# Row maxima and V's bound through TensorE in 16 bits, and a constant moved into exp's bias

## The chip, the cores and the metric

One Trainium2 chip; the kernel runs on one of its cores. The metric is the time of one execution on the device, in microseconds. A core has TensorE (PE in the profile; its weight loads are shown apart as PEld), VectorE (DVE), ScalarE (ACT), GpSimd (POOL) and SyncE (SP, which issues the DMAs here).

## What is computed

Attention over 16 heads of 64 columns (2 batches of 8), with the queries averaged in pairs, and then two MLPs over the 1152 rows that come out, all in float32:

```
q_pool = q.reshape(B, H, S // 2, 2, D).mean(axis=3)
scores = matmul(q_pool, k^T) / sqrt(D)
scores = scores - max(scores, axis=-1)
attn   = exp(scores);  attn = attn / (sum(attn) + 1e-09)
x      = matmul(attn, v)                       # then heads side by side: 1152 x 512
h = x @ w_in;   x = (max(h, 0) + alpha * min(h, 0)) @ moe_w_out
h = x @ w2_in;  out = (P(h) / (Q(h) + 1e-06)) @ moe2_w_out
```

S is 1152, so a head has 576 pooled queries against 1152 keys. The change lies in the attention.

## The kernel before

Heads are worked two at a time (8 pairs). Near-float32 precision comes from splitting operands in a high and a low part and multiplying the parts. A head's keys are taken in NT = 9 tiles of 128, its queries in NJ = 5 blocks of 128 (the last one of 64).

Before a pair's scores are made, the maximum over the keys is found for every query. `max_mm` (line 435) multiplies query blocks with the keys in three chunks of 384 (tiles m0, m1, m2 in PSUM, nine steps a pair); ScalarE's `max_relu` (441) and VectorE's `max_1` (444) and `max_2` (449) reduce them to `nm`. `max_split` (463 to 467) then makes the negative maximum of 5 or 9 query blocks at once, adds a constant (exp's factor 2^14, as PSH / SC), and splits it in a high and a low part `mt` of two columns per block. `max_rows` (481) turns each block's two columns into two rows with a TensorE transpose against the float32 identity, and `max_put` (497) copies these rows to partitions 64 and 65 of `QQ`, from where they are two more rows of the second matmul of the scores, against two rows of ones in `K2`. So the scores come out with the maximum already subtracted. For the first head `first_m` (511) does the work of `max_rows` and `max_put`.

`score` (523) makes the scores of one key tile: four matmuls to a PSUM buffer `st`, of which there are two. `p_exp` (534) is ScalarE's exp of it to `PF`, `p_lo` (540) the low part `PL` on GpSimd (on VectorE for some tiles), and `av` (552 to 556) multiplies both, in 16 bits, with V's high and low part: fifteen small matmuls a tile, some three tiles after the scores.

V is scaled by a power of two. `v_abs` (360) sums |V| of a head per partition to `AM`; `v_max` (372) turns the two heads' columns into a row by a product with the identity, in float32; `v_scale` (377 to 382) takes the maximum and makes a power of two and its inverse from it; `v_scale2` (385) spreads the two over all partitions by a product with a row of ones, in float32; `v_scale3` (390) copies them.

The order on each engine is the order of the program: every step is entered with a time on a scale of one key tile per unit (`at(time, fn, ...)`), and `emit` sorts by it. The engines run these lists in order, with semaphores between them. During the last pair the weights of the MLPs are unpacked as well (lines 128 to 156) by ScalarE, VectorE and GpSimd. `init_1` and `init_2` set constants at the start; `warm` (245) runs products of the identity with itself.

Of the kernel before, what the change touches and what calls it, by code (L numbers as in the profile page):

```python
# [11 lines left out]
F32 = mybir.dt.float32  # L12
F32R = mybir.dt.float32r
F16 = mybir.dt.float16
BF16 = mybir.dt.bfloat16
I32 = mybir.dt.int32
I64 = mybir.dt.int64
AF = mybir.ActivationFunctionType
ALU = mybir.AluOpType
AX = mybir.AxisListType  # L20

P = 128
# [3 lines left out]
def attention_then_two_mlps(  # L26
# [14 lines left out]
    nc = tc.nc  # L41
    NPAIR, _, _, SQ = qT.shape
    BH, D = 2 * NPAIR, P // 2
# [6 lines left out]
    HALF = SQ // 2  # L50
# [5 lines left out]
    SC = 0.5 / math.sqrt(D)  # L56
    PSH = 14.0 * math.log(2.0)
# [135 lines left out]
    for f in range(NF):  # L193
# [10 lines left out]
    hold = actx.enter_context(tc.tile_pool(name="hold", bufs=1))  # L204
# [5 lines left out]
    small = actx.enter_context(tc.tile_pool(name="small", bufs=2))  # L210
# [3 lines left out]

    CW = 384
    EVEN, ODD = 2, 3
    K1 = [[(early, hold, early)[i].tile([P, SK + CW], F32R, name=f"K1_{o}{i}")
           for i in range((EVEN, ODD)[o])] for o in range(2)]  # L220
    QQ = [[(early, hold, early)[i].tile([P, 2, SQP], F32R, name=f"QQ_{o}{i}")
           for i in range((EVEN, ODD)[o])] for o in range(2)]
    K2 = [[(early, hold)[i].tile([D + 2, SK], F32R, name=f"K2_{o}{i}") for i in range(2)] for o in range(2)]
    V16 = [hold.tile([P, NT, 130], F16, name=f"V16_{i}") for i in range(2)]
    NPB = 6
    PF = [hold.tile([P, SQP], F32, name=f"PF_{i}") for i in range(NPB)]
    PL = [hold.tile([P, SQP], F16, name=f"PL_{i}") for i in range(NPB)]
    ident = hold.tile([P, P], F32, name="ident")
    ones1 = hold.tile([1, P], F32, name="ones1")
    PAD = SQP - SQ  # L230

    def init_1():
        for o in range(2):
            for qq in QQ[o]:
                z = slice(0, PAD) if o else slice(SQ, SQP)
                nc.gpsimd.memset(qq[:, 0, z].bitcast(F32), 0.0)
        make_identity(nc, ident)
        nc.gpsimd.memset(ones1, 1.0)


    def warm(n):
# [5 lines left out]
    def init_2():  # L247
        for i in range(2):
            for o in range(2):
                e = nc.vector if o > i else nc.gpsimd  # L250
                e.memset(K2[o][i][D:D + 2, :].bitcast(F32), 1.0)
        for i in range(NPB):
            nc.vector.memset(PF[i][:, SQ:SQP], 0.0)
            nc.vector.memset(PL[i][:, SQ:SQP], 0.0)
        for i in range(2):
            nc.gpsimd.memset(V16[i][:, :, 0:1], 1.0)

    def of(bufs, n):
        p, o = divmod(n, 2)
        return bufs[o][p % len(bufs[o])]  # L260
# [4 lines left out]
    KR, QR, QS, QH, QL, KH, KL, VR, VS, AM, X, NM, O, ST, TS = ({} for _ in range(15))  # L265
# [21 lines left out]
    def k_hi(p, c=slice(0, SK)):  # L287
        if p not in KH:
            KH[p] = prep.tile([P, SK + CW], F32R, tag="kh", name="kh")
        nc.scalar.activation(out=KH[p][:, c], in_=KR[p][:, c], func=AF.Copy)  # L290

    def k_diff(p):
        nc.gpsimd.tensor_tensor(
            out=KH[p][:, SK:SK + CW], in0=KH[p][:, CW:2 * CW].bitcast(F32),
            in1=KH[p][:, 0:CW].bitcast(F32), op=ALU.subtract)

# [41 lines left out]
    def first_kh():  # L338
        for c in (slice(0, 2 * CW), slice(2 * CW, SK)):
            nc.scalar.activation(out=of(K1, 0)[0:D, c], in_=KR[0][0:D, c], func=AF.Copy)  # L340
# [4 lines left out]
    def first_kd():  # L345
        k = of(K1, 0)
        nc.vector.tensor_tensor(
            out=k[:, SK:SK + CW], in0=k[:, CW:2 * CW].bitcast(F32), in1=k[:, 0:CW].bitcast(F32),
            op=ALU.subtract)
# [14 lines left out]
    VC = NJ * (D + 1)  # L364

    def v_max(p):
        if p:
            AM[p, 1] = O[2 * p - 2]
        else:
            AM[p, 1] = psum.tile([P, 512], F32, tag="o", name="vt")  # L370
        for o in range(2):
            nc.tensor.matmul(AM[p, 1][0:1, VC:VC + P], lhsT=AM[p][:, o:o + 1], rhs=ident,
                             start=p == 0 and o == 0, stop=o == 1, skip_group_check=True)

    def v_scale(p):
# [6 lines left out]
        nc.vector.reciprocal(out=g[:, 4:5], in_=g[:, 3:4])  # L382

    def v_scale2(p):
        nc.tensor.matmul(AM[p, 1][:, VC + P:VC + P + 2], lhsT=ones1, rhs=AM[p, 0][:, 3:5], start=p == 0,
                         stop=True, skip_group_check=True)

    def v_scale3(p):
# [3 lines left out]
    def v_scale_at(t1, t2, p):  # L392
        at(t1, v_max, p)
        at(t1 + 0.2, v_scale, p)
        at(t2, v_scale2, p)
        at(t2 + 0.2, v_scale3, p)
# [20 lines left out]
    NJ2 = 2 * NJ - 1  # L417
# [42 lines left out]
    def max_split(p, j0, j1):  # L460
        w = j1 - j0
        nm1 = small.tile([P, NJ2], F32, tag="nm1", name="nm1")
        nc.vector.tensor_reduce(
            out=nm1[:, 0:w], in_=NM[p][:, j0:j1, :], axis=AX.X, op=ALU.max, negate=True)
        TS[p, j0] = mt = small.tile([P, 2, NJ2], F32R, tag="mt", name="mt")
        nc.vector.tensor_scalar(mt[:, 0, 0:w], nm1[:, 0:w], PSH / SC, None, op0=ALU.add)
        nc.vector.scalar_tensor_tensor(
            out=mt[:, 1, 0:w], in0=nm1[:, 0:w], scalar=PSH / SC, in1=mt[:, 0, 0:w].bitcast(F32),
            op0=ALU.add, op1=ALU.subtract)

    def max_rows(p, j0, j1):
        mt = TS.pop((p, j0))
        parts = {}
        for tag, k0, k1 in (("m0", 0, NJ - 1), ("m1", NJ - 1, NJ), ("m2", NJ, NJ2)):
            k0, k1 = max(k0, j0), min(k1, j1)
            if k0 < k1:
                tp = psum.tile([P, 512], F32, tag=tag, name="mtp")
                for j in range(k0, k1):  # L480
                    nc.tensor.transpose(  # L481
                        out=tp[0:2, (j - k0) * P:(j - k0 + 1) * P], in_=mt[:, :, j - j0].bitcast(F32),
                        identity=ident)
                parts[k0] = tp, (k1 - k0) * P
        TS[p, j0] = parts

# [14 lines left out]
    def max_fin_at(time, *a):  # L501
        at(time, max_split, *a)
        at(time + (0.621 if a[0] == 0 else 1.129), max_rows, *a)
        at(time + (0.922 if a[0] == 0 else 1.4), max_put, *a)


    def first_m():
        mt, q = TS.pop((0, 0)), of(QQ, 0)
        st = stp.tile([P, 2, 512], F32, tag="st", name="mst")
        for j in range(NJ):  # L510
            nc.tensor.transpose(
                out=st[0:2, j // 4, j % 4 * P:(j % 4 + 1) * P], in_=mt[:, :, j].bitcast(F32), identity=ident)
        nc.scalar.activation(out=q[D:D + 2, 1, 0:512], in_=st[0:2, 0, :], func=AF.Copy)
        nc.scalar.activation(out=q[D:D + 2, 1, 512:SQ], in_=st[0:2, 1, 0:SQ - 512], func=AF.Copy)

# [11 lines left out]
    def buf(n, t):  # L527
        return (n * NT + t) % NPB

    def top(u):  # L530
        return PF[u].bitcast(BF16).rearrange("p (q two) -> p q two", two=2)[:, :, 1]

    def p_exp(n, t):
        nc.scalar.activation(  # L534
            out=PF[buf(n, t)][:, 0:SQ].rearrange("p (h q) -> p h q", h=2),
            in_=ST.pop((n, t))[:, :, 0:HALF], func=AF.Exp, scale=SC)

    def p_lo(n, t, e):
        u = buf(n, t)
        e.tensor_tensor(out=PL[u][:, 0:SQ], in0=PF[u][:, 0:SQ], in1=top(u)[:, 0:SQ], op=ALU.subtract)  # L540

    def av(n, t):
        i = n % 2
        u = buf(n, t)
        if t == 0:
            O[n] = psum.tile([P, 512], F32, tag="o", name="o")
        for j in range(NJ):
            o = O[n][:, j * (D + 1):(j + 1) * (D + 1)]
            ph = top(u)[:, j * P:(j + 1) * P]
            pl = PL[u][:, j * P:(j + 1) * P]  # L550
            first, last = t == 0 and j == 0, t == NT - 1
            nc.tensor.matmul(o, lhsT=ph, rhs=V16[i][:, t, 0:D + 1], start=first, stop=False,  # L552
                             skip_group_check=True)
            nc.tensor.matmul(o[:, 1:D + 1], lhsT=ph, rhs=V16[i][:, t, D + 1:2 * D + 1], start=False,  # L554
                             stop=False, skip_group_check=True)
            nc.tensor.matmul(o, lhsT=pl, rhs=V16[i][:, t, 0:D + 1], start=False, stop=last,  # L556
                             skip_group_check=True)
# [96 lines left out]
    for p in range(NP):  # L654
# [21 lines left out]
        for o in range(2):  # L676
            n = 2 * p + o
# [167 lines left out]
    def mt(s):  # L845
        return S2 * NP + 1 + 3.3 * s


    def dly(s):
        if s < PASS_B:  # L850
            return 2.5
        return 3.5

    for s, u in enumerate(steps):
# [23 lines left out]
        e = mt(s + dly(s))  # L878
# [18 lines left out]
    t = PASS_B + 1.8  # L897
# [48 lines left out]
```

## Time and profile before

| | |
|---|---|
| median of 3 runs | 686.64 us (685.75 to 687.48) |
| the profiled execution | 682.94 us, of which the span of the instructions is 681.1 |
| TensorE / VectorE busy | 647.6 us (95%) / 516.2 us (76%) |
| ScalarE / GpSimd busy | 485.4 us (71%) / 403.8 us (59%) |
| mean granted clock of TensorE | 0.987 |
| chain that ended last | TensorE 64%, VectorE 20%, ScalarE 7% |

Busy time of TensorE counts matmuls whose ends are modelled and which overlap in its pipeline: two rows of matmuls are told apart by their starts. In a timeline, pieces of one line that follow each other without a gap stand in one row with their count; its length reaches from the first start to the last end.

### The profile page before, as it was taken

The numbers are of one execution on the slowest core, as the hardware profiler recorded it, in microseconds if no ns is written. First come the engines' busy times: TensorE is split into PE (matmuls) and PEld (weight loads), VectorE is DVE, ScalarE is ACT, GpSimd is POOL, SyncE is SP. The second block draws the span as 40 slices with busy tenths as digits, with TensorE's granted clock in tenths as the row PEclk, the third lists the DMA queues.
The fourth block names the chain that finished last, engine by engine and source line by source line (L and its number), as shares of the span: only waits on it lengthen the run. The fifth ranks groups of instructions, "written<-read, shape, count | busy, mean of one in ns | idle before, by whom it ended". The sixth has DMA issues, their size and how long they took to land.

```text
span 681.1 us, 13756 instructions
## 1 busy us (share of the span) xinstructions
PE 647.6 (95%) x5226; PEld 580.3 (85%) x5226; DVE 516.2 (76%) x944; ACT 485.4 (71%) x916; POOL 403.8 (59%) x352
## 2 busy tenths in 40 slices
PE   6888999999999889999999999999999999999997
PEld 4767898988989779999999999999887779999995
DVE  7677867778678998998992149996788877667774
ACT  5666686776867756665764368888788888778774
POOL 8454776857766766685663226785465655444442
PEclk9699999999999979999999999999999999999999
DMA  8979659496593224343330005640320010001001
GB/s 221 197 197 226 129 159 216 125 230 129 160 207 103 69 89 155 125 153 125 140 136 35 1 1 195 231 161 31 124 93 31 1 47 0 2 1 47 1 1 46
DMA packets 21537, 73.96 MB, mean 109 GB/s; under 512 B 3232, under 2 KB 3232, under 8 KB 21472
## 3 DMA queue, kind: packets, MB, share of 16 engines
q1 hardware_dynamic: 21472, 73.10, 37.7%
q8 instruction: 41, 0.67, 0.4%
q14 instruction: 24, 0.20, 0.1%
HBM read 47.72 MB, written 2.36 MB: 74 GB/s over the span
## 4 chain that ended last, share of the span: by engine, by line
PE 64%; DVE 20%; ACT 7%; issue 5%; DMA 2%; POOL 1%; SPq 1%; POOLq 0%; DVEq 0%; ACTq 0%
PE hp L184 20%; PE acc L810 18%; PE st L523 10%; PE m L435 6%; DVE bits L138 3%; PE o L552 3%; PE o L554 2%; PE o L556 2%; DVE bits L133 2%; DVE ring L146 2%; DVE g L791 1%; DVE g L776 1%; DVE hp L789 1%; DVE b L787 1%; PE mtp L481 1%
## 5 line engine op out<-in xcount | busy, mean ns | idle before, releaser
L540 POOL TENSOR_TENSOR PL<-PF 128x576 f16<-128x576 f32 x106 | 134.8, 1284 | 77.1 <-ACT PF L534 75.3
L799 POOL TENSOR_TENSOR gl<-g,gh 128x384 fp32r<-128x384 f32 x96 | 104.8, 1092 | 72.2 <-ACT gh L795 58.4
L534 ACT ACTIVATE PF<-st 128x576 f32<-128x576 f32 x144 | 92.2, 650 | 43.9 <-PE st L523 42.2
L810 PE MATMUL acc<-woh,gl 128*128 128x512 f32 x288 | 114.3, 397 | 3.2 <-POOL gl L799 3.2
L810 PE MATMUL acc<-woh,gh 128*128 128x512 f32 x288 | 113.3, 393 | 2.2 <-ACT m L841 1.7
L810 PE MATMUL acc<-wol,gh 128*128 128x512 f32 x288 | 113.2, 393 | 0.0
L523 PE MATMUL st<-QQ,K 128*128 128x288 f32 (+1 forms) x576 | 105.6, 311 | 0.4 <-ACT PF L534 0.4
L769 POOL TENSOR_TENSOR b<-a,b 128x384 f32<-128x384 f32 x48 | 48.9, 1019 | 84.4 <-ACT b L757 83.3
L523 PEld LDWEIGHTS st<-QQ,K 128*128 128x128 f32 (+1 forms) x576 | 90.3, 197 | 2.6 <-ACT V L407 1.3
L184 PE MATMUL hp<-xh,wih 128*128 128x384 f32 x384 | 83.7, 340 | 0.0
L184 PE MATMUL hp<-xl,wih 128*128 128x384 f32 x384 | 83.2, 338 | 0.0
L184 PE MATMUL hp<-xh,wil 128*128 128x384 f32 x384 | 83.0, 338 | 0.0
L435 PE MATMUL m<-K,QQ 128*128 128x384 f32 x234 | 70.5, 372 | 8.9 <-DVE nm L444 5.1
L552 PE MATMUL o<-V,PF 128*128 128x65 f16 x720 | 76.7, 195 | 1.6 <-DVE x L567 1.4
L556 PE MATMUL o<-V,PL 128*128 128x65 f16 x720 | 75.5, 193 | 1.9 <-DVE PL L540 1.7
L554 PE MATMUL o<-V,PF 128*128 128x64 f16 x720 | 76.0, 196 | 0.0
L184 PEld LDWEIGHTS hp<-xh,wih 128*128 128x128 f32 x384 | 69.4, 188 | 7.5
L552 PEld LDWEIGHTS <-PF 128*128 128x128 bf16 x720 | 66.5, 98 | 9.1 <-issue 2.1
L795 ACT ACTIVATE gh<-g 128x384 fp32r<-128x384 f32 x96 | 49.9, 520 | 31.8 <-DVE g L760 21.8
L556 PEld LDWEIGHTS <-PL 128*128 128x128 f16 x720 | 67.6, 100 | 2.3 <-DVE PL L540 1.9
L810 PEld LDWEIGHTS acc<-woh,gl 128*128 128x128 f32 x288 | 54.1, 188 | 18.2 <-POOL gl L799 6.8
L184 PEld LDWEIGHTS hp<-xh,wil 128*128 128x128 f32 x384 | 68.7, 188 | 0.0
(151 smaller groups left out, 1404.6 us busy)
## 6 DMA issues: line engine op xcount, KB each, us to landing
K<-kh SPq DMA_DIRECT2D x30, 384.0 KB, 5.2
ring<-in_w SPq DMA_DIRECT2D x19, 512.0 KB, 3.6
raw<-in_w SPq DMA_DIRECT2D x13, 512.0 KB, 3.5
ring<-in_w1o SPq DMA_DIRECT2D x10, 512.0 KB, 3.4
vr<-in_v SPq DMA_DIRECT2D x8, 576.0 KB, 5.5
ring<-in_w2o SPq DMA_DIRECT2D x9, 512.0 KB, 3.5
QQ<-qh SPq DMA_DIRECT2D x15, 288.0 KB, 6.4
qr<-in_qT SPq DMA_DIRECT2D x7, 576.0 KB, 6.6
```

Of the source, the lines that this page charges most:

```text
L184: nc.tensor.matmul(hp, lhsT=w_[:, c * P:(c + 1) * P], rhs=x_[:, c, ts], start=k == 0, stop=k == 3 * KT - 1)
L435: nc.tensor.matmul(s[:, 0:CW], lhsT=of(QQ, n)[:, 0, k * P:(k + 1) * P], rhs=of(K1, n)[:, k0:k0 + CW], start=n == parts[0][0], stop=n == pa ...
L523: nc.tensor.matmul(st[:, hf, 0:HALF], lhsT=k_[:, ks], rhs=q_[:, c:c + HALF], start=first, stop=not first)
L534: nc.scalar.activation(out=PF[buf(n, t)][:, 0:SQ].rearrange("p (h q) -> p h q", h=2), in_=ST.pop((n, t))[:, :, 0:HALF], func=AF.Exp, scale=SC)
L540: e.tensor_tensor(out=PL[u][:, 0:SQ], in0=PF[u][:, 0:SQ], in1=top(u)[:, 0:SQ], op=ALU.subtract)
L552: nc.tensor.matmul(o, lhsT=ph, rhs=V16[i][:, t, 0:D + 1], start=first, stop=False, skip_group_check=True)
L554: nc.tensor.matmul(o[:, 1:D + 1], lhsT=ph, rhs=V16[i][:, t, D + 1:2 * D + 1], start=False, stop=False, skip_group_check=True)
L556: nc.tensor.matmul(o, lhsT=pl, rhs=V16[i][:, t, 0:D + 1], start=False, stop=last, skip_group_check=True)
L769: nc.gpsimd.tensor_tensor(out=E[u, "b"], in0=E[u, "a"], in1=E[u, "b"], op=ALU.mult)
L795: nc.scalar.activation(out=G[u][0], in_=E[u, "g"], func=AF.Copy)
L799: nc.gpsimd.tensor_tensor(out=gl, in0=E[u, "g"], in1=gh.bitcast(F32), op=ALU.subtract)
L810: nc.tensor.matmul(acc, lhsT=g_[:, cs], rhs=w_, start=f == 0 and k == 0, stop=f == NF - 1 and k == 2)
```

## The change

- `max_split` multiplies the negative maximum by 2^-15 and makes both parts float16. The first op is a TENSOR_TENSOR with a column of `consts` (2^-15, repeated) instead of a TENSOR_SCALAR with an immediate. The two rows of `K2` are 2^15 instead of 1.
- `max_rows` and `first_m` use plain matmuls with a float16 identity, `ident16`, instead of transposes with the float32 one.
- The constant 2^14 is no longer added to the maximum: `p_exp` has it as its bias, a column of `consts`.
- `v_max` takes the upper 16 bits of the sums, as bfloat16, against `ident16`; `v_scale2` takes the powers of two as bfloat16 against float16 ones.
- `init_1` and `init_2` set the two columns of `consts`, the float16 identity and the new values.

```diff
@@ tiles and constants
-    ones1 = hold.tile([1, P], F32, name="ones1")
+    ident16 = hold.tile([P, P], F16, name="ident16")
+    ones1 = hold.tile([1, P], F16, name="ones1")
+    consts = hold.tile([P, 2], F32, name="consts")
+    shift, down = consts[:, 0:1], consts[:, 1:2]
+    MS = 2.0 ** 15
@@ init_1
+        nc.gpsimd.memset(shift, PSH)
+        nc.gpsimd.memset(down, 1.0 / MS)
@@ init_2
-                e.memset(K2[o][i][D:D + 2, :].bitcast(F32), 1.0)
+                e.memset(K2[o][i][D:D + 2, :].bitcast(F32), MS)
...
+        nc.vector.tensor_copy(ident16, ident)
...
+    def top(x):
+        return x.bitcast(BF16).rearrange("p (q two) -> p q two", two=2)[:, :, 1]
@@ v_max
-            nc.tensor.matmul(AM[p, 1][0:1, VC:VC + P], lhsT=AM[p][:, o:o + 1], rhs=ident,
+            nc.tensor.matmul(AM[p, 1][0:1, VC:VC + P], lhsT=top(AM[p])[:, o:o + 1], rhs=ident16,
@@ v_scale2
-        nc.tensor.matmul(AM[p, 1][:, VC + P:VC + P + 2], lhsT=ones1, rhs=AM[p, 0][:, 3:5], start=p == 0,
+        nc.tensor.matmul(AM[p, 1][:, VC + P:VC + P + 2], lhsT=ones1, rhs=top(AM[p, 0])[:, 3:5], start=p == 0,
@@ max_split
-        TS[p, j0] = mt = small.tile([P, 2, NJ2], F32R, tag="mt", name="mt")
-        nc.vector.tensor_scalar(mt[:, 0, 0:w], nm1[:, 0:w], PSH / SC, None, op0=ALU.add)
+        TS[p, j0] = mt = small.tile([P, 2, NJ2], F16, tag="mt", name="mt")
+        nc.vector.tensor_tensor(
+            out=mt[:, 0, 0:w], in0=nm1[:, 0:w], in1=down.to_broadcast([P, w]), op=ALU.mult)
         nc.vector.scalar_tensor_tensor(
-            out=mt[:, 1, 0:w], in0=nm1[:, 0:w], scalar=PSH / SC, in1=mt[:, 0, 0:w].bitcast(F32),
-            op0=ALU.add, op1=ALU.subtract)
+            out=mt[:, 1, 0:w], in0=nm1[:, 0:w], scalar=1.0 / MS, in1=mt[:, 0, 0:w],
+            op0=ALU.mult, op1=ALU.subtract)
@@ max_rows (first_m alike)
-                    nc.tensor.transpose(
-                        out=tp[0:2, (j - k0) * P:(j - k0 + 1) * P], in_=mt[:, :, j - j0].bitcast(F32),
-                        identity=ident)
+                    nc.tensor.matmul(tp[0:2, (j - k0) * P:(j - k0 + 1) * P], lhsT=mt[:, :, j - j0],
+                                     rhs=ident16, start=True, stop=True)
@@ p_exp
-            in_=ST.pop((n, t))[:, :, 0:HALF], func=AF.Exp, scale=SC)
+            in_=ST.pop((n, t))[:, :, 0:HALF], func=AF.Exp, scale=SC, bias=shift)
```

No instruction changes its place among the others. On TensorE the 16-bit matmuls have a weight load of their own in the list. V's maximum in the middle of a pair (`am` is `AM`, `st` the scores, `m` the maxima) stood so before:

```order
L523 MATMUL st<-QQ_107,K_00_102 128x288 x2
L523 MATMUL st<-QQ_107,K_00_112 128x288 x2
L435 MATMUL m_1685<-K_01_103,QQ_108 128x384
L372 MATMUL o<-ident,am 1x128 x2
L523 MATMUL st<-QQ_107,K_00_102 128x288 x2
L523 MATMUL st<-QQ_107,K_00_112 128x288 x2
```

and with the change (its lines are numbered some twelve higher):

```order
L535 MATMUL st<-QQ_107,K_00_102 128x288 x2
L535 MATMUL st<-QQ_107,K_00_112 128x288 x2
L447 MATMUL m_1690<-K_01_103,QQ_108 128x384
L384 LDWEIGHTS am
L384 MATMUL o<-ident_131,am 1x128
L384 LDWEIGHTS am
L384 MATMUL o<-ident_131,am 1x128
L535 MATMUL st<-QQ_107,K_00_102 128x288 x2
L535 MATMUL st<-QQ_107,K_00_112 128x288 x2
```

The neighbours are the same. Each of the two products now has its load ahead of it.

## Rows read from the trace of the kernel before

**Rows 1.** The page, part 1: busy time (share of the span) and instructions of TensorE.

```profile
PE 647.6 (95%) x5226; PEld 580.3 (85%) x5226; DVE 516.2 (76%) x944; ACT 485.4 (71%) x916; POOL 403.8 (59%) x352
```

**Rows 2.** Waits, longest first: engine, line <- releaser: us in total, times, longest.

```profile
ACT PF L534 <- PE st L523: 42.2, 59, 2.7
...
PE st L523 <- ACT PF L534: 0.4, 1, 0.4
```

**Rows 3.** Chain in order of time, two head pairs: start us, us, what.

```profile
109.24 0.44 PE m L435
...
112.47 1.14 PE mtp L481 x9
...
140.88 1.14 PE mtp L481 x9
```

**Rows 4.** Timeline of PE, one set of transposes: start us, us, engine line op.

```profile
112.47 1.14 PE L481 MATMUL mtp<-ident,mt 128*2 128x128 f32 x9
...
114.10 0.19 PE L552 MATMUL o<-V,PF 128*128 128x65 f16 x1
...
114.19 0.19 PE L552 MATMUL o<-V,PF 128*128 128x65 f16 x1
```

**Rows 5.** Timeline of PE around V's bound, same columns.

```profile
124.90 0.34 PE L435 MATMUL m<-K,QQ 128*128 128x384 f32 x1
125.07 0.69 PE L523 MATMUL st<-QQ,K 128*128 128x288 f32 x4
125.61 0.34 PE L435 MATMUL m<-K,QQ 128*128 128x384 f32 x1
...
126.41 0.80 PE L523 MATMUL st<-QQ,K 128*128 128x288 f32 x4
...
129.12 0.70 PE L523 MATMUL st<-QQ,K 128*128 128x288 f32 x4
129.75 0.38 PE L385 MATMUL o<-g,ones 1*128 1x2 f32 x2
130.06 0.61 PE L435 MATMUL m<-K,QQ 128*128 128x384 f32 x2
```

**Rows 6.** Groups by line and shape: xcount | busy us, mean ns | idle before.

```profile
L534 ACT ACTIVATE PF<-st 128x576 f32<-128x576 f32 x144 | 92.2, 650 | 43.9 <-PE st L523 42.2 <-POOL idm masks.py:199 0.3
...
L757 ACT ACTIVATE g<-hp,na 128x384 f32<-128x384 f32 x48 | 31.4, 654 | 0.0
...
L757 ACT ACTIVATE b<-hp 128x384 f32<-128x384 f32 x48 | 23.1, 480 | 17.4 <-PE hp L184 17.4
...
L481 PE MATMUL mtp<-ident,mt 128*2 128x128 f32 x69 | 9.0, 272 | 5.4 <-DVE mt L467 5.4
...
L372 PE MATMUL o<-ident,am 128*1 128x128 f32 x28 | 4.2, 272 | 0.0
```

**Rows 7.** Timeline of POOL and of DVE at the end of a pair's maxima.

```profile
106.41 1.70 POOL L540 TENSOR_TENSOR PL<-PF 128x576 f16<-128x576 f32 x1 [0.53 <-ACT PF L534]
...
111.03 1.15 POOL L540 TENSOR_TENSOR PL<-PF 128x576 f16<-128x576 f32 x1 [1.31 <-ACT PF L534]
...
107.02 1.70 DVE L540 TENSOR_TENSOR PL<-PF 128x576 f16<-128x576 f32 x1
...
111.72 0.48 DVE L466 TENSOR_SCALAR mt<-nm 128x9 fp32r<-128x9 f32 x1
```

**Rows 8.** Timeline of POOL and DVE, the first pair's split.

```profile
14.25 2.60 POOL L300 TENSOR_TENSOR kr<-kr,kh 64x1152 fp32r<-64x1152 f32 x1
...
14.33 2.55 DVE L466 TENSOR_SCALAR mt<-nm 128x5 fp32r<-128x5 f32 x1
```

**Rows 9.** Chain in order of time, the start of the kernel.

```profile
24.00 0.51 PE vt L385 x2
...
32.34 5.51 DMA vr<-in_v
```

**Rows 10.** Busy time by stretch, the last pair: us, each engine, PEclk, DMA, GB/s.

```profile
250.00:252.00 2.00, 2.00 (x24) 1.85 (x22) 2.00 (x3) 0.76 (x2) 0.71 (x2) 0.50 0.04 8
```

More of the change, by code (lines that the diff above doesn't have):

```diff
@@ L510, in first_m @@
         for j in range(NJ):
-            nc.tensor.transpose(
-                out=st[0:2, j // 4, j % 4 * P:(j % 4 + 1) * P], in_=mt[:, :, j].bitcast(F32), identity=ident)
+            nc.tensor.matmul(st[0:2, j // 4, j % 4 * P:(j % 4 + 1) * P], lhsT=mt[:, :, j], rhs=ident16,
+                             start=True, stop=True)
         nc.scalar.activation(out=q[D:D + 2, 1, 0:512], in_=st[0:2, 0, :], func=AF.Copy)
@@ L528, in buf @@
         return (n * NT + t) % NPB
-    def top(u):
-        return PF[u].bitcast(BF16).rearrange("p (q two) -> p q two", two=2)[:, :, 1]
     def p_exp(n, t):
@@ L535, in p_exp @@
             out=PF[buf(n, t)][:, 0:SQ].rearrange("p (h q) -> p h q", h=2),
-            in_=ST.pop((n, t))[:, :, 0:HALF], func=AF.Exp, scale=SC)
+            in_=ST.pop((n, t))[:, :, 0:HALF], func=AF.Exp, scale=SC, bias=shift)
     def p_lo(n, t, e):
         u = buf(n, t)
-        e.tensor_tensor(out=PL[u][:, 0:SQ], in0=PF[u][:, 0:SQ], in1=top(u)[:, 0:SQ], op=ALU.subtract)
+        e.tensor_tensor(out=PL[u][:, 0:SQ], in0=PF[u][:, 0:SQ], in1=top(PF[u])[:, 0:SQ], op=ALU.subtract)
     def av(n, t):
@@ L548, in av @@
             o = O[n][:, j * (D + 1):(j + 1) * (D + 1)]
-            ph = top(u)[:, j * P:(j + 1) * P]
+            ph = top(PF[u])[:, j * P:(j + 1) * P]
             pl = PL[u][:, j * P:(j + 1) * P]
```

## The prediction

> **What bounds the kernel now.** I read the page's busy shares, then the waits, then the chain of work that ended last, and at the three places of the change the timeline. TensorE is busy for 95% of the span [rows 1]. The waits say who holds whom in the attention part: ScalarE waits 42.2 us for scores before its exps, while TensorE waits for an exp once, for 0.4 us [rows 2]. So the scores set the pace and the exps follow. The chain agrees: the nine row-maximum transposes of one head pair begin at 112.47 and those of the next at 140.88, so a pair takes 28.4 us, and between them the chain stays on TensorE except where a maximum's matmul waits for VectorE just before 109.24 [rows 3]. From about 61 to 216 us, then, time taken out of TensorE's stream is time saved. The ends are different. Up to 37.85 us the chain waits for loads [rows 9]. From about 216 to 260 us, the last pair, VectorE is split between the pair and the MLP weights; TensorE stops there, and its clock is granted at 0.50, the 1.2 GHz level, in some stretches [rows 10]. After that the MLPs run, which the change does not touch.
>
> **Transposes of the maxima.** The nine start at 112.47 and their row is 1.14 us long, of which 0.27 is the last one's own length, the mean of its kind, so one follows another after (1.14 - 0.27)/8 = 0.109 us [rows 4, 6]. They become plain float16 matmuls of the same 128 columns. The nearest float16 row is the product with V: three matmuls (65, 64 and 65 columns, each with a weight load of its own) start at 114.10 and the next three at 114.19, 0.09 us for 194 columns [rows 4]. By columns 128 take 0.059, which saves 0.05 each and **0.45 us a pair**. The lower bound is nothing, if something other than the columns paces them at 0.109. I take the float16 row, because it has the same types and a load per matmul.
>
> **V's bound.** A float32 product of 128 columns stands as two pieces in the trace, so the two products of line 372 are four pieces. A maximum's matmul is followed by the next matmul after 0.17 us (124.90 to 125.07); behind the one at 125.61 the scores would start at 125.78 and start at 126.41. Their four take 0.80 instead of 0.69, since their weights cannot be loaded ahead [rows 5]. The bound costs 0.63 + 0.11 = 0.74 us. Two float16 passes of 0.059 and the same 0.11 make 0.23, so up to 0.5 is saved; some wait ahead of it may stay, and I take **0.45**. The lower bound is 0.22, two of four pieces at 0.109. Line 385 spreads two values over the partitions: the scores at 129.12 would leave TensorE free at 129.12 + 0.54 = 129.66 (0.54 as from 125.07 to 125.61), and the next matmul starts at 130.06 [rows 5]. With the same 0.10 of late weights that is 0.50. One pass instead of two, and a 16-bit load of the ones, should leave 0.15: **0.35 saved**, with a lower bound of 0.2, half of the 0.40.
>
> **Exp's bias.** All 144 exps now read a bias from SBUF, an operand per partition. The trace has the price: from PSUM, 384 elements take 480 ns with immediates and 654 with two such operands, 87 for each [rows 6]. An exp goes from 650 to about 740 ns, and 144 x 0.09 = 13 us come onto ScalarE. Most of it is covered, because ScalarE idles 42.2 us waiting for the scores [rows 2]. What is not covered are chains of fixed length from a score to a wait of TensorE. There are two a pair. One: an exp releases the GpSimd subtraction at 106.41; VectorE's subtraction at 107.02, with two SBUF operands, lasts 1.70 because it can only run once GpSimd's ends at 108.11; then comes the maximum for which the matmul at 109.24 waits [rows 3, 7]. Two: an exp releases the GpSimd subtraction at 111.03, which ends at 112.18, the split's first op waits for that end, and the transposes at 112.47 for the split [rows 4, 7]. I charge 0.09 for each, 0.18 a pair; the bounds are nothing and all 13 us.
>
> **The other op in the split.** The TENSOR_SCALAR of line 466 starts at 111.72 and ends at 112.20, just behind the GpSimd op [rows 7]; at the start the same op lasts 2.55 us, behind a GpSimd op that ends at 16.85 [rows 8]. The new TENSOR_TENSOR reads two operands from SBUF, as VectorE's subtraction at 107.02 does, and that one waited just so [rows 7]. I take no change: 0. The upper bound of a gain is the wait.
>
> **The rest.** The float16 identity is one more copy on VectorE, which at that time waits for the first load; two more one-column memsets stand on GpSimd ahead of work that is not waited for; the rows set to 2^15 were set before too. All of that is hidden behind the loads, and would cost a few tenths without them. No DMA is added, and no queue's order changes.
>
> **The sum.** In the steady stretch lie five sets of nine transposes and six bounds (the 28 pieces of line 372 are seven bounds [rows 6], one of them before 61 us): 5 x 0.45 + 6 x (0.45 + 0.35) = 7.05. The exps give back 5 x 0.18 = 0.9. At the start, line 385 stands on the chain with 0.51 us, ahead of the load of V that ends at 37.85 [rows 9]: 0.4 saved. Between 38 and 61 us another bound (0.8) and ten transposes (0.5) are saved, but TensorE waits for VectorE several times there, so I count 0.4. In the last pair I charge 0.4 for exps on the path. Together 7.05 - 0.9 + 0.4 + 0.4 - 0.4 = **6.55 us**. The profiled execution took 682.94 us (span 681.1 and 1.84 around it), the median of the runs is 686.64; I take the difference off the median: **680.1 us**. In the profile this would be a span of 674.5. A change within 0.3%, 2.06 us, cannot be told from none.
>
> **The rivals.**
> *The small matmuls do not get faster.* The change would then do only half of what it says: the transposes stay at 0.109, and of each bound 0.25 and 0.25 are saved. That leaves 6 x 0.5 - 0.9 + 0.7 - 0.4 = 2.4, 684.2 us. For it: a weight load of two columns with a matmul has no float16 row here. Against it: the products with V go at 0.03 each, loads of 128 columns included [rows 4]. The Trainium skill, "TensorE: Matmul & The Clock Gate", section "Back-to-back issue gap", gives about 81 ns per matmul for a stream of loads and matmuls of 128 columns; by that figure 0.25 instead of 0.45 would be saved on a set of transposes and 0.04 less on a bound, 5.3 in all, 681.3 us, and the 0.03 of the products with V does not decide it, as those are half as wide.
>
> *The split is no longer held by GpSimd.* If the second operand, one value repeated, does not count as a second read of SBUF, the split's two ops take 0.17 each. Then TensorE's wait before the transposes goes (0.2 to 0.3 a pair, 1.3 in all), about 1 us each at 60 and at 226 us, and TensorE no longer waits out the first split's 2.55 us [rows 8]: half of that, 1.3, since loads bound that stretch. 680.1 - (1.3 + 2 + 1.3) = 675.5 us. Against it stands the row at 107.02.
>
> *The saving is taken back.* TensorE runs ahead into waits for VectorE and GpSimd, whose work has not shrunk, or a further stretch of the last pair falls to the 1.2 GHz level. The length of such stretches (some 2 to 4 us) sets the price: another one or two lose 2 to 4 us, with 2 us of new waits 5.5: 685.6 us. Against it: the pairs repeat with one such wait each.
>
> *The exps become the bound (slower).* If ScalarE falls behind, TensorE waits for free score buffers, and each exp adds its 0.09. Without the 0.9 and 0.4 already charged the saving is 7.85, so this wins once more than 87 of the 144 exps are on the path; with all of them 686.64 - 7.85 + 13 = 691.8 us. For it: exp stands in ScalarE's queue ahead of the maxima's relu. Against it: the 42.2 us of idle time [rows 2].
>
> **How the numbers follow.** The forecast has 0.53 (its own range 678.5 to 682.5), small matmuls no faster 0.13, the split freed 0.12, the saving taken back 0.14, the exps 0.08. The range, 676.0 to 685.0, takes in the forecast, most of the second, half of the third and the better part of the fourth. Faster by over 0.3%: 0.53 + 0.12 + about 0.08 of the second and 0.03 of the fourth, 0.76; slower: the exps and a little of the fourth, 0.09; the same 0.15.
>
> **What would show it.** Right: nine transposes start within 0.5 us, not 0.9; exps of about 740 ns; the pair's period near 27.3 instead of 28.4; the split's first op still ending with a GpSimd op. Wrong: a row of waits of TensorE for exps of several us; the period unchanged with VectorE on the chain; new stretches at the 1.2 GHz level.

## The result and the profile after

The changed kernel takes **690.96 us** (median of 4 runs, 690.49 to 692.39) against 686.55 for the kernel before (4 runs): a ratio of 1.0067, interval 1.0048 to 1.0087. It is 4.4 us slower, where 6.55 us of gain were forecast. The profiled execution took 692.39 us (span 690.3). That of before took 682.94, which is 3.6 below its median, so the distance between the two profiles is about twice that between the kernels; what follows goes by the steady pairs (from about 61 to 207 us), where a kernel's pairs can be compared one by one.

The page, part 1, answers to [rows 1]: TensorE's share fell by one point, though its matmuls became fewer and the changed ones shorter.

```profile
PE 648.9 (94%) x5202; PEld 583.4 (85%) x5202; DVE 525.2 (76%) x945; ACT 495.5 (72%) x916; POOL 407.4 (59%) x354
```

The waits, longest first (engine, line <- releaser: us in total, times, longest):

```profile
ACT PF L543 <- PE st L535: 42.1, 49, 2.1
...
PE m L447 <- DVE nm L456: 10.3, 8, 1.6
```

ScalarE still has its 42 us of idle time [rows 2], so the exps did not become the bound. The second row is the news: TensorE waits for VectorE's reduction `max_1` 10.3 us in all, 1.6 at most. The same row of before, which the prediction did not read, shows half of that:

```profile
PE m L435 <- DVE nm L444: 5.1, 6, 0.9
```

The chain in order of time, two head pairs (start us, us, what), answers to [rows 3]:

```profile
108.22 1.70 DVE PL L549
109.92 0.48 DVE nm L456
110.44 0.45 PE m L447
...
114.90 0.86 PE mtp L494 x9
...
143.48 0.67 PE mtp L494 x9
```

The nine matmuls that turn the maxima begin at 114.90 and again at 143.48: this pair lasts 28.6 us. From first score to first score, two of the five steady pairs last 28.5 us and three 29.7 to 30.0; before, all last 28.4 to 28.5.

The timeline of TensorE, one such pair (start us, us, engine line op; in brackets the idle time before and who ended it), answers to [rows 4, 5]:

```profile
110.44 0.45 PE L447 MATMUL m<-K,QQ 128*128 128x384 f32 x1 [1.56 <-DVE nm L456]
...
112.01 0.24 PE L563 MATMUL o<-V,PF 128*128 128x64 f16 x1
112.06 0.24 PE L565 MATMUL o<-V,PL 128*128 128x65 f16 x1
...
116.38 0.20 PE L563 MATMUL o<-V,PF 128*128 128x64 f16 x1
116.41 0.19 PE L565 MATMUL o<-V,PL 128*128 128x65 f16 x1
...
128.19 0.27 PE L384 MATMUL o<-ident,am 128*1 128x128 f16 x2
128.40 0.80 PE L535 MATMUL st<-QQ,K 128*128 128x288 f32 x4
...
131.73 0.17 PE L397 MATMUL o<-g,ones 1*128 1x2 bf16 x1
131.84 0.62 PE L447 MATMUL m<-K,QQ 128*128 128x384 f32 x2
...
143.48 0.67 PE L494 MATMUL mtp<-ident,mt 128*2 128x128 f16 x9
144.08 0.80 PE L535 MATMUL st<-QQ,K 128*128 128x288 f32 x4
```

The small matmuls are short: V's bound takes 0.21 us to the scores at 128.40, its spreading 0.11 to the matmul at 131.84, the transposes 0.60 to the scores at 144.08. But TensorE stood idle for 1.56 us ahead of the matmul at 110.44, which is the one before which the chain of before waited [rows 3], for about 0.85 us. After that pause it runs slowly: its small products follow each other by 0.05 us at 112 and by 0.03 at 116. The stretches (us, busy time and instructions of PE, PEld, DVE, ACT, POOL, then PEclk, DMA share, GB/s) say why:

```profile
110.00:112.00 2.00, 1.56 (x11) 1.49 (x12) 1.93 (x7) 0.48 (x1) 0.93 (x1) 1.00 1.03 243
112.00:116.00 4.00, 4.00 (x46) 3.61 (x46) 2.50 (x8) 1.94 (x4) 1.15 (x1) 0.57 0.97 205
140.00:144.00 4.00, 3.75 (x53) 3.40 (x53) 3.83 (x13) 1.97 (x3) 1.79 (x2) 1.00 1.00 225
```

The granted clock fell to the 1.2 GHz level for some 3.4 us of the stretch from 112 to 116. That happened behind three of the five pauses of the steady pairs (at 81, 112 and 170 us), and not behind those at 140 and 198; these three are the pairs of 29.7 to 30.0 us. Before, it never happened between 60 and 215 us.

The exps cost what was forecast, 743 ns against 650 [rows 6]. This is the row by line and shape (xcount | busy us, mean ns | idle before):

```profile
L543 ACT ACTIVATE PF<-st,consts 128x576 f32<-128x576 f32 x144 | 104.4, 743 | 45.6 <-PE st L535 42.1 <-POOL PL L549 3.2
```

So TensorE's stream is shorter, and its pause longer. Where the pause comes from is read on VectorE and GpSimd, at the place of [rows 7]. First before (start us, us, engine line op, idle before):

```profile
102.01 3.87 POOL L540 TENSOR_TENSOR PL<-PF 128x576 f16<-128x576 f32 x3
108.48 1.24 POOL L540 TENSOR_TENSOR PL<-PF 128x576 f16<-128x576 f32 x1 [0.38 <-ACT PF L534]
...
105.67 1.43 DVE L300 TENSOR_TENSOR ring<-ring,kh 128x1152 fp32r<-128x1152 f32 x1
108.64 0.55 DVE L444 TENSOR_REDUCE nm<-m 128x1 f32<-128x384 f32 x1
```

and after:

```profile
103.22 7.71 POOL L549 TENSOR_TENSOR PL<-PF 128x576 f16<-128x576 f32 x5
112.33 1.15 POOL L549 TENSOR_TENSOR PL<-PF 128x576 f16<-128x576 f32 x1 [1.41 <-ACT PF L543]
...
106.17 2.13 DVE L312 TENSOR_TENSOR ring<-ring,kh 128x1152 fp32r<-128x1152 f32 x1
108.22 1.70 DVE L549 TENSOR_TENSOR PL<-PF 128x576 f16<-128x576 f32 x1
109.84 0.54 DVE L456 TENSOR_REDUCE nm<-m 128x1 f32<-128x384 f32 x1
110.31 0.54 DVE L461 CUSTOM_DVE_ANT_0 junk<-m,relu 128x384 bf16<-128x384 f32 x1
```

Before, GpSimd waited for an exp from 105.88 to 106.41, and VectorE's subtraction of the next keys (`k_lo`, line 300) began 0.2 us ahead of that hole and took 1.43 us; GpSimd's next subtraction, from 106.41, took 1.70 where one alone takes 1.15 (the row at 111.03 in [rows 7]). After, GpSimd's five subtractions `p_lo` follow each other for 7.71 us without a gap. `k_lo` comes into the middle of them and takes 2.13, the `p_lo` on VectorE behind it 1.70 as before, and `max_1`, for which TensorE waits, comes only then. The forecast knew the second of these two subtractions; the first was in nobody's sum.

### The profile page after: what moved, and what is told of

Same layout as the page of the kernel before. It is cut to its first block, busy times and chain, and to the rows that moved or that the text cites. A ratio compares the mean times of both kernels' runs of the same rounds, so it can differ in the third digit from the quotient of the medians.

```text
span 690.3 us, 13709 instructions
## 1 busy us (share of the span) xinstructions
PE 648.9 (94%) x5202; PEld 583.4 (85%) x5202; DVE 525.2 (76%) x945; ACT 495.5 (72%) x916; POOL 407.4 (59%) x354
## 4 chain that ended last, share of the span: by engine, by line
PE 63%; DVE 23%; ACT 6%; issue 5%; DMA 1%; POOL 1%; SPq 0%; POOLq 0%; DVEq 0%; ACTq 0%
PE hp L184 19%; PE acc L819 18%; PE st L535 9%; PE m L447 6%; DVE bits L138 3%; PE o L561 3%; PE o L563 3%; PE o L565 3%; DVE PL L549 2%; DVE bits L133 2%; DVE ring L146 2%; DVE g L800 1%; DVE g L785 1%; DVE hp L798 1%; DVE b L796 1%
## 5 line engine op out<-in xcount | busy, mean ns | idle before, releaser
L549 POOL TENSOR_TENSOR PL<-PF 128x576 f16<-128x576 f32 x106 | 137.8, 1316 | 80.6 <-ACT PF L543 80.0
L543 ACT ACTIVATE PF<-st,consts 128x576 f32<-128x576 f32 x144 | 104.4, 743 | 45.6 <-PE st L535 42.1
L535 PE MATMUL st<-QQ,K 128*128 128x288 f32 (+1 forms) x576 | 108.6, 317 | 0.5 <-ACT PF L543 0.5
L535 PEld LDWEIGHTS st<-QQ,K 128*128 128x128 f32 (+1 forms) x576 | 92.6, 201 | 3.1 <-ACT PF L543 1.0
L447 PE MATMUL m<-K,QQ 128*128 128x384 f32 x234 | 72.0, 379 | 16.9 <-DVE nm L456 10.3
L565 PE MATMUL o<-V,PL 128*128 128x65 f16 x720 | 78.9, 196 | 3.6 <-DVE PL L549 3.6
L561 PE MATMUL o<-V,PF 128*128 128x65 f16 x720 | 80.1, 198 | 1.9 <-DVE x L576 1.3
L563 PE MATMUL o<-V,PF 128*128 128x64 f16 x720 | 79.4, 199 | 0.0
L561 PEld LDWEIGHTS <-PF 128*128 128x128 bf16 x720 | 68.5, 100 | 9.3 <-issue 2.3
L565 PEld LDWEIGHTS <-PL 128*128 128x128 f16 x720 | 69.5, 102 | 4.2 <-DVE PL L549 4.0
L563 PEld LDWEIGHTS <-PF 128*128 128x128 bf16 x720 | 69.6, 101 | 0.6 <-issue 0.6
```

Of the source, the lines that this page charges most:

```text
L447: nc.tensor.matmul(s[:, 0:CW], lhsT=of(QQ, n)[:, 0, k * P:(k + 1) * P], rhs=of(K1, n)[:, k0:k0 + CW], start=n == parts[0][0], stop=n == pa ...
L535: nc.tensor.matmul(st[:, hf, 0:HALF], lhsT=k_[:, ks], rhs=q_[:, c:c + HALF], start=first, stop=not first)
L543: nc.scalar.activation(out=PF[buf(n, t)][:, 0:SQ].rearrange("p (h q) -> p h q", h=2), in_=ST.pop((n, t))[:, :, 0:HALF], func=AF.Exp, scale ...
```

## The experiments

Each ratio is to the kernel before, run beside it (medians of 686.3 to 686.9 us). Two measures come back in all of them. **A pair** is the time from the first score of the third pair to that of the seventh, divided by four. **The pause** is TensorE's idle time ahead of that one matmul, in each of the five steady pairs. In before they are 28.4 and 0.85 us; in the changed kernel 29.1 (28.45 where there is no slow stretch) and 1.54 to 1.57.

The theories at the start: (A) the shorter stream and the longer exps together make the pause longer, and the clock that falls behind it costs the rest; (B) TensorE's shorter stream alone does it; (C) the exps alone do; and last, the split's new op does. After the first four runs came theory (E): what TensorE's stream saves in a pair is lost again to the stretch in which VectorE's and GpSimd's subtractions hold each other up, so that a pair cannot get shorter by it.

### The change without exp's bias

```diff
-            in_=ST.pop((n, t))[:, :, 0:HALF], func=AF.Exp, scale=SC, bias=shift)
+            in_=ST.pop((n, t))[:, :, 0:HALF], func=AF.Exp, scale=SC)
@@ max_put (first_m alike)
-                            func=AF.Copy)
+                            func=AF.Copy, bias=PSH / SC / MS / 2)
```

The constant goes into the two rows as an immediate of the copy that is made anyway.

> The changed kernel without exp's bias; the constant 2^14 is added in ScalarE's copy of the two rows instead, as an immediate. Theory A (later exps and an earlier TensorE together push GpSimd's subtractions into VectorE's subtraction of the keys, so that the last maxima of a pair come late; the longer stall then lets TensorE's clock fall): exps back at 650 ns, the stall at the ninth maximum step of a pair back from 1.55 us of idle to 0.85 or less, no stretch at 1.2 GHz between 60 and 215 us, and 679 to 682 us. Theory B (TensorE's shorter stream alone does it): stall of 1.5 us as in the changed kernel, 688 to 691. Theory C (the longer exps alone do it): 679 to 682, as A; the next run tells these apart.

686.73 us, ratio 0.9997 (0.9981 to 1.0012). A pair takes 28.1 us, the pause is 1.38, and the clock falls behind none of these five pauses. So the bias costs some 4 us of the change's time. But without it nothing is gained either: TensorE's shorter stream alone makes most of the longer pause. The time is neither theory A's 679 to 682 us nor B's 688 to 691.

### The kernel before with exp's bias alone

```diff
-            in_=ST.pop((n, t))[:, :, 0:HALF], func=AF.Exp, scale=SC)
+            in_=ST.pop((n, t))[:, :, 0:HALF], func=AF.Exp, scale=SC, bias=shift)
...
```

In the split, zero takes the place of the constant.

> The kernel before with exp's bias alone (zero is added in the split instead of the constant). Theory A: exps 743 ns, the stall grows by 0.1 to 0.3 us a pair, at most one new stretch at 1.2 GHz: 687 to 690 us. Theory B: 686 to 687.5. Theory C: stalls of 1.5 us a pair and three or four new stretches at 1.2 GHz, 692 to 697, since nothing is saved on TensorE.

689.74 us, ratio 1.0043 (1.0027 to 1.0059). A pair takes 28.7, the pause is 1.03, and there is no slow stretch in the steady pairs. The exps alone cost about 3 us, 0.3 a pair where 0.18 were charged. By themselves they made no slow stretch there.

### The split's first op as it was

```diff
-        nc.vector.tensor_tensor(
-            out=mt[:, 0, 0:w], in0=nm1[:, 0:w], in1=down.to_broadcast([P, w]), op=ALU.mult)
+        nc.vector.tensor_scalar(mt[:, 0, 0:w], nm1[:, 0:w], 1.0 / MS, None, op0=ALU.mult)
```

> The changed kernel with a TENSOR_SCALAR as the first op of the split again (product with 2^-15, float16 out). All theories A to C: no difference beyond 0.7 us from 691, since both ops end with the GpSimd op that runs when they start. Theory D (the two-operand op is what disturbs GpSimd and VectorE): 685 to 688.

691.13 us, ratio 1.0061 (1.0033 to 1.0088), the pauses 1.53 to 1.56. The op does nothing to the time: with nine columns it lasts 648 ns as TENSOR_SCALAR and 667 as TENSOR_TENSOR on average, and in both cases it ends with the GpSimd subtraction that runs when it starts (112.92 + 0.59 beside 112.33 + 1.15 in the changed kernel).

### Work for TensorE in the pause

```diff
             TS[p, j, c] = s
+            if p > 1 and j == NJ2 - 1 and c == 1:
+                for _ in range(40):
+                    nc.tensor.matmul(O[max(O)][:, 456:512], lhsT=ident16, rhs=ident16[:, 0:56], start=False,
+                                     stop=True, skip_group_check=True)
```

Forty small products go to columns of the output bank that nothing reads.

> The changed kernel with 40 added float16 products of 128x56, into columns that nobody reads, ahead of the matmul that stalls at the end of each pair's maxima (pairs 2 to 7). If the fall of TensorE's clock after the stall costs what the profile suggests (three stretches of 3.4 us at half clock between 81 and 174 us, some 1.5 us each): no such stretch in 60 to 215 us, and 685 to 688 us. If the stall alone costs: 690.5 to 692, the stall itself staying and the added products taking some of its idle time.

686.10 us, ratio 0.9992 (0.9975 to 1.0008). TensorE's timeline round the pause:

```profile
109.51 1.21 PE L448 MATMUL o<-ident 128*128 128x56 f16 x40
111.22 0.44 PE L451 MATMUL m<-K,QQ 128*128 128x384 f32 x1 [0.50 <-DVE nm L460]
```

The wait is no shorter (1.21 of products and 0.50 idle), but the clock falls behind none of the five, and a pair takes 28.45. That gives back about 5 us: this is the price of the slow stretches, 1.3 to 1.6 us for each of three in the steady pairs and the rest behind them (the seventh pair lasts 33.25 us in the changed kernel, with two such stretches, and 30.4 here, with none). What is left of the pause still takes up the whole saving, together with the longer exps, since the time is then just that of before.

### Half of TensorE's saving at a time

First the transposes alone: the change without exp's bias, and V's bound back in float32.

```diff
-            nc.tensor.matmul(AM[p, 1][0:1, VC:VC + P], lhsT=top(AM[p])[:, o:o + 1], rhs=ident16,
+            nc.tensor.matmul(AM[p, 1][0:1, VC:VC + P], lhsT=AM[p][:, o:o + 1], rhs=ident,
...
```

The spreading goes back in the same way.

> The float16 transposes without the bias (constant in the copy of the rows) and with V's bound in float32 as before. Theory E (from the middle of a pair to the stall, GpSimd's subtractions and VectorE's two-operand ops follow each other without a gap, and TensorE's saving on V's bound, which lies in that stretch, only lengthens the stall; the transposes lie behind the stall and count): the same as the run without bias, 685.5 to 688, with the stall at 0.85 us of idle. The forecast's sum, in which each saving counts: V's bound is missing, so 4 to 5 us slower than the run without bias, 690 to 692.

686.51 us, ratio 0.9995 (0.9975 to 1.0016); a pair 28.1, the pause 0.85 as before. The transposes come through, with 0.27 a pair (28.38 to 28.11).

Then V's bound alone, in the kernel before:

```diff
-            nc.tensor.matmul(AM[p, 1][0:1, VC:VC + P], lhsT=AM[p][:, o:o + 1], rhs=ident,
+            nc.tensor.matmul(AM[p, 1][0:1, VC:VC + P], lhsT=top(AM[p])[:, o:o + 1], rhs=ident16,
...
```

The spreading goes with it.

> The kernel before with V's bound alone in 16 bits. Theory E: the stall grows from 0.85 to 1.3 to 1.5 us of idle and the pair keeps its 28.4 us; 686 to 688.5, the upper end if TensorE's clock falls after the longer stall. The forecast's sum: 6 x 0.8 saved, 682 us.

687.33 us, ratio 1.0019 (1.0006 to 1.0033): if anything slower. A pair takes 28.4 as before, and the pause has grown from 0.85 to between 1.38 and 1.40. The timelines of TensorE, GpSimd and VectorE (the last two a pair later):

```profile
109.40 0.44 PE L440 MATMUL m<-K,QQ 128*128 128x384 f32 x1 [1.38 <-DVE nm L449]
...
130.59 7.71 POOL L542 TENSOR_TENSOR PL<-PF 128x576 f16<-128x576 f32 x5
...
133.70 1.97 DVE L305 TENSOR_TENSOR kr<-kr,kh 128x1152 fp32r<-128x1152 f32 x1
```

0.52 us are saved in the bound (0.32 and 0.20, taken apart below), and by 0.53 us the pause is longer. GpSimd's two short waits for exps (0.53 and 0.38 us in before) are gone, as in the changed kernel, and `k_lo` takes 1.97 instead of 1.42: the scores come earlier, but the subtractions behind them end no earlier. The transposes stand behind the pause, at the pair's end; the bound stands ahead of it, in the middle. That fits theory E, but does not yet show what makes the pause.

### One subtraction from GpSimd to VectorE

```diff
-    ON_DVE = (3, 9, 13, 14)
+    ON_DVE = (3, 7, 9, 13)
```

In the changed kernel:

> The changed kernel with one GpSimd subtraction moved: tile 7's low part on VectorE instead of tile 14's. Theory E: GpSimd gets 1.15 us free in the stretch that bounds the end of the maxima, so the stall falls from 1.55 to under 0.8 us of idle, no stretch at 1.2 GHz between 60 and 215 us, 683 to 687 us. If the longer exps bound the pair (theory C): no gain, 690 to 692.

687.79 us, ratio 1.0032 (1.0015 to 1.0049). In the version without exp's bias:

> The same move in the kernel without exp's bias. Theory E: the stall is nearly gone and the savings of the 16-bit matmuls come through: 679 to 683 us, 4 to 7 below the run without bias. If the stall's cause lies elsewhere: 686 to 688.

688.08 us, ratio 1.0034 (1.0016 to 1.0052). GpSimd's row is broken up, but VectorE now has one more subtraction in the same stretch: TensorE waits twice a pair, 0.65 and 0.78 us in the first kernel, 0.49 and 0.77 in the second. In the changed kernel the clock falls behind none of these shorter pauses, and it is some 3 us faster; a pair takes 28.6 and 28.3 us, no less than the 28.45 and 28.1 without the move. Theory E had forecast 683 to 687 and 679 to 683, so both went against it as it was put. They leave the same work in the same stretch, one subtraction more of it on VectorE, and so do not say whether that work makes the pause; the next runs do.

### The subtraction of the keys moved out of the stretch

```diff
-        at(k + 0.9, k_lo, p, nc.vector)
-        at(k + 2.4, k2_move, e)
+        kl = k + 0.9 if p == 2 else S2 * (p - 2) + 15.0
+        at(kl, k_lo, p, nc.vector)
+        at(kl + 1.5, k2_move, e)
...
-        at(max(k + 2.4, S2 * (p - 1) + 0.356), k2_move, o)
+        at(max(kl + 1.5, S2 * (p - 1) + 0.356), k2_move, o)
```

`k_lo` of the next pair but one is not urgent. Five of them go from tile 10 of a pair to tile 15, where GpSimd stands idle. On TensorE, GpSimd and ScalarE no instruction changes its place, and on VectorE these five alone; the copies of their results (`k2_move`) go with them. Three kernels have this: the change without exp's bias, the kernel before, and the change whole.

> The changed kernel without exp's bias (686.7 us, a pair 28.1, TensorE's stall in each pair 1.38), with VectorE's subtraction of the next keys moved from tile 10 of a pair to tile 15 in five pairs: from the stretch where VectorE's and GpSimd's subtractions hold each other up to one in which GpSimd stands idle for 3.7 us. If the saving in TensorE's stream is lost to that stretch, the stall all but goes (under 0.4) and the saving of V's bound comes through: a pair 26.9 to 27.4 us, 680 to 683.5. If TensorE is held by something else in a pair, the stall moves elsewhere, a pair stays at 28.0 or more, and the time is 685.5 to 688.

677.71 us, ratio 0.9863 (0.9841 to 0.9886); a pair 26.5, no pause over 0.25 us in the five pairs.

> The kernel before, with the same subtraction moved in the same five pairs and nothing else. If the collision of the subtractions is what TensorE waits for, before's own stall of 0.85 us a pair goes: a pair 27.6 to 27.9, 682.5 to 685. If before was paced by TensorE's stream alone and the stall is only slack, it stays at 685.5 to 687.5.

681.26 us, ratio 0.9920 (0.9896 to 0.9944); a pair 27.3, no pause.

> The whole change, with the same subtraction moved. With the stall of 1.56 us gone the granted clock should not fall between 60 and 215 us, and a pair should last about 0.2 to 0.5 longer than without the bias: 27.2 to 27.8, 682 to 685.5. If the time lost by the change lies in the longer exps and not in the stall and the clock, it stays at 688.5 to 691.

678.13 us, ratio 0.9869 (0.9845 to 0.9892); a pair 26.67, no pause. VectorE and GpSimd in this last kernel, at the same place of a pair:

```profile
103.59 1.53 DVE L549 TENSOR_TENSOR PL<-PF 128x576 f16<-128x576 f32 x1
105.04 0.55 DVE L456 TENSOR_REDUCE nm<-m 128x1 f32<-128x384 f32 x1
...
109.89 1.35 DVE L312 TENSOR_TENSOR ring<-ring,kh 128x1152 fp32r<-128x1152 f32 x1
```

```profile
100.64 5.49 POOL L549 TENSOR_TENSOR PL<-PF 128x576 f16<-128x576 f32 x4
106.49 1.15 POOL L549 TENSOR_TENSOR PL<-PF 128x576 f16<-128x576 f32 x1 [0.36 <-ACT PF L543]
107.93 1.15 POOL L549 TENSOR_TENSOR PL<-PF 128x576 f16<-128x576 f32 x1 [0.29 <-ACT PF L543]
112.90 5.69 POOL L549 TENSOR_TENSOR PL<-PF 128x576 f16<-128x576 f32 x5 [3.83 <-ACT PF L543]
```

`k_lo` runs at 109.89 in 1.35 us, while GpSimd waits from 109.08 to 112.90. GpSimd's row has gaps again, and `max_1` comes with one subtraction ahead of it instead of two. Over the steady stretch (columns as in the stretches above) TensorE of before, of the change, and of the change with `k_lo` moved:

```profile
62.00:200.00 138.00, 133.68 (x1910) 121.11 (x1910) 104.10 (x257) 103.49 (x200) 96.22 (x77) 1.00 0.69 166
```

```profile
62.00:200.00 138.00, 130.13 (x1819) 118.68 (x1818) 108.41 (x250) 104.66 (x193) 99.16 (x76) 0.96 0.65 160
```

```profile
62.00:200.00 138.00, 137.52 (x2013) 126.67 (x2012) 112.54 (x270) 115.46 (x213) 101.36 (x83) 1.00 0.75 178
```

TensorE was idle for 4.3 us of these 138 before, for 7.9 with the change, and for 0.5 now, when it is at last what the prediction took it for: the engine that sets the pace. Theory E holds: in all three kernels the pause went with `k_lo`. All three times lie below their forecasts, in part because more was lost in the pause than its idle time: a pair of before became 1.1 us shorter, with a pause of 0.85. The place shows in TensorE's timeline, first of before and then with `k_lo` moved:

```profile
107.97 0.42 PE L435 MATMUL m<-K,QQ 128*128 128x384 f32 x1
109.24 0.44 PE L435 MATMUL m<-K,QQ 128*128 128x384 f32 x1 [0.84 <-DVE nm L444]
109.52 0.29 PE L523 MATMUL st<-QQ,K 128*128 128x288 f32 x1
```

```profile
108.55 0.59 PE L435 MATMUL m<-K,QQ 128*128 128x384 f32 x2
108.98 0.29 PE L523 MATMUL st<-QQ,K 128*128 128x288 f32 x1
```

From the start of the first of these two matmuls to the scores it is 1.55 us and 0.43, and that is the 1.1. Without the wait the second starts while the first still runs; idle time, which counts from the first one's end, leaves that out. From tile to tile the rest of the pair is the same in both kernels to within 0.01 us.

With the pause gone, both savings on TensorE come through: 27.27 to 26.46 us a pair without exp's bias is 0.81, beside the 0.27 of the transposes and the 0.52 of the bound. The change is then worth 3.1 us (681.26 to 678.13), and without exp's bias 3.6; these two cannot be told apart by their intervals. What no run separates is `k_lo`'s own 1.35 us from the time for which GpSimd holds it: moving it takes both out of VectorE's row ahead of `max_1`.

## Why the prediction was wrong

| kernel | median us | a pair | pause | pair less pause |
|---|---|---|---|---|
| before | 686.6 | 28.4 | 0.85 | 27.55 |
| transposes alone | 686.5 | 28.1 | 0.85 | 27.25 |
| V's bound alone | 687.3 | 28.4 | 1.39 | 27.0 |
| change without exp's bias | 686.7 | 28.1 | 1.38 | 26.7 |
| the change | 691.0 | 29.1 | 1.56 | – |
| before, `k_lo` moved | 681.3 | 27.3 | – | 27.3 |
| the change, `k_lo` moved | 678.1 | 26.7 | – | 26.7 |
| change without bias, `k_lo` moved | 677.7 | 26.5 | – | 26.5 |

**The step that failed** is the sentence "From about 61 to 216 us, then, time taken out of TensorE's stream is time saved". The row beside it spoke against it: the chain of before left TensorE once a pair, before 109.24 [rows 3], for a `max_1` that stood behind two subtractions. TensorE's work ahead of such a wait can shrink without the wait's end coming earlier, and here that end is set by `k_lo` and `p_lo` on VectorE, which take 2.13 and 1.70 us among GpSimd's subtractions. The bound's 6 x (0.45 + 0.35) = 4.8 us of the sum lay ahead of that wait, and in the steady pairs none of it arrived. With the bias, the longer pause (1.56 us) was also followed by the slow stretches, for which the sum had no term in the steady pairs.

**Transposes, 0.45 a pair.** Right in kind: the measured gain is 0.27 a pair (28.38 to 28.11). The timeline of TensorE in before shows what the step left out:

```profile
140.88 1.14 PE L481 MATMUL mtp<-ident,mt 128*2 128x128 f32 x9
141.77 0.77 PE L523 MATMUL st<-QQ,K 128*128 128x288 f32 x4
```

The last transpose is 0.27 long and began at 141.75, so the scores followed it within 0.02 us. After the change the last one is 0.23 long (the mean of line 494) and begins at 143.48 + 0.67 - 0.23 = 143.92, and the scores start at 144.08, 0.16 later. The spacing of the nine is (0.67 - 0.23)/8 = 0.055 us, a little better than the 0.059 of the forecast; but the work behind them no longer follows at once. From the first of the nine to the scores it is 0.89 before and 0.60 after, which is that gain to within 0.02. By the 81 ns that the Trainium skill, "TensorE: Matmul & The Clock Gate", section "Back-to-back issue gap", gives for a stream of loads and matmuls of 128 columns, the nine would be 0.081 us apart; here, where a load has two columns, the trace has 0.055, and it decides.

**V's bound, 0.80 a pair.** The timeline of before has the bound itself, which the step had priced by its neighbours:

```profile
125.88 0.60 PE L372 MATMUL o<-ident,am 128*1 128x128 f32 x4
126.41 0.40 PE L523 MATMUL st<-QQ,K 128*128 128x288 f32 x1
```

From 125.88 to 126.41 are 0.53 us, and 0.21 after: 0.32 saved, not 0.45. The 0.10 from 125.78, when TensorE was free, to 125.88 are there after the change too. The spreading went from 0.31 (129.75 to 130.06 in [rows 5]) to 0.11: 0.20 saved, not 0.35, which is the lower bound of the step. Together 0.52 a pair, as the stream in the table shows (27.55 to 27.0). The term was a third too large, and in the change it was worth nothing.

**Exp's bias, 0.18 a pair.** The 93 ns are right, and the two chains of fixed length were the right place to look. Through the collision they cost 0.3 a pair (before with the bias alone); with `k_lo` out of the way 0.21 (26.67 against 26.46), close to the forecast.

**The split's op, 0.** Right: its first op still ends with GpSimd's, and the old op in its place gives the same time. **The start, 0.4 and 0.4.** The first is not seen: the first head's ninth score stands at 38.2 us after and 37.7 before. There the loads bound [rows 9], which the step said itself. The second cannot be settled: from that score to the second pair's first it is 22.2 us after and 23.3 before, and between 22.7 and 25.1 in the profiles of the other kernels.

**The last pair, -0.4.** It can't be settled. From the seventh pair's first score to the first matmul of the MLPs it is 56.9 us in the profile of before, 61.9 in that of the change and 58.2 to 62.2 in the others; so the profile that the step was read from was the shortest of all.

**The rivals.** "The saving is taken back" named both ways in which it went, waits for VectorE and stretches at 1.2 GHz, and put them at 685.6, because it looked for the stretches in the last pair. All stretches together cost about 5 us (690.96 against 686.10 with the pause filled), most of it in the steady pairs. "Against it: the pairs repeat with one such wait each" should have been read the other way: such a wait in each pair can grow in each pair. "The exps become the bound" came out at about the right time for the wrong reason: TensorE waits for an exp once, for 0.5 us. "The small matmuls do not get faster" falls with the spacing of 0.055 us, and "the split is no longer held by GpSimd" with the op that still ends with GpSimd's.

## What to carry to other kernels

A stage is paced by an engine only if nothing on another engine stands in its chain. Where the chain leaves the busiest engine once per period, even for 0.85 us in 28, what is shortened ahead of that wait may only make it longer, as here, and the first thing to look at is the work that holds the waited-for engine. An unurgent operation that another engine holds up is worth trying where that engine is idle. Here one subtraction moved by five tiles was worth 5.3 us by itself, and turned a change that cost 4.4 us into one that gained 3.1.

## What the runs showed of the hardware

**Pauses and the clock.** Behind a pause of 1.56 us TensorE's granted clock fell to the 1.2 GHz level in three of five cases, 0.8 to 1.6 us after the pause's end, for 3.4 us (in two of five with the split's old op). Behind the five of 1.38 us in the version without the bias, and the five of 0.85 before, it did not fall. A pause of 1.5 to 1.6 us at 60 to 63 us stands in all thirteen profiles, and in two of them the clock fell within 0.7 us of its end. With forty needless products of 56 columns in each of the five pauses the clock stayed up there; the kernel was about 5 us faster.

**VectorE and GpSimd in turns.** `k_lo`, with both operands in SBUF, took 1.35 us with GpSimd idle and 2.13 among its subtractions; `p_lo` on VectorE 0.75 and 1.70. The split's first op took 667 ns on average as a multiplication by one repeated value and 648 with an immediate, so this does not show that the repeated operand is what makes it wait.
